# Batch 5's loads requested behind the transpose of the first pairs' last rows, on the same queue

## The chip, the cores and the metric

One core of one Trainium2 chip. The metric is the device time of one execution in microseconds; repeats are given as medians. Each run carries a state: slow when it is over 1.5% above the fastest run of the same kernel, unknown when there is only one.

## The reference, cut to what matters

Linear attention, then an MLP mixer, over 8 batches of 576 rows and 512 columns:

```python
q_p, k_p = phi(q), phi(k)                       # phi(x) = elu(x) + 1
kv  = einsum('bhsd,bhse->bhde', k_p, v)
x   = einsum('bhsd,bhde->bhse', q_p, kv) / den  # attention, 8 heads of 64
u   = x + (relu(x^T w_tok1) w_tok2)^T           # token mixing
out = u + relu(u w_ch1) w_ch2                   # channel mixing, 512 -> 1536 -> 512
```

## The kernel before

The loop runs one pass per batch n. TensorE does the channel mixing of batch n (`mm3`, `mm4`) while, in between, the attention and the token mixing of batch n + 1 and the phi of batch n + 2 are filled in. Each batch has 4 full row groups of 128 and a tail of 64 rows; the tails of two batches share one tile `ut`. Operands that TensorE needs transposed are made by DMA transposes on SyncE's queue: `uT` from `u`, `qT` from phi(q), `uTt` from `ut`. The loads of q, k and v go through the same queue.

```python
def load(nm, n, c, gate=None):                  # 576 KB, two of them for each of q, k, v
    ...
    return after(nc.sync.dma_start(out=raw[nm, n % 2][:, js], in_=src_[:, js]), gate)

def utr_tail_dma(p):                            # "utt"
    nc.sync.dma_start_transpose(out=uTt, in_=ut[p % 2])

def mm3_tail(i):                                # reads uTt, line L517, from step 12 of the next pass
    ...
            nc.tensor.matmul(out=ps[:, m], lhsT=wc1[:, kj, ...], rhs=uTt[:, kj, :], ...)

def nd_mm(n, c, rs):                            # reads qT, line L210, from step 2 of a pass
    ...

AT3 = {..., "mm2t": 15, "uta": 12, "utb": 13, "utt": 15}          # steps in pass n = 2
for n in range(2, B):
    ...
        fill += [(12 + d, lambda: qtr_dma(n + 2))]                # qT, two transposes
        if n == 2:
            fill += [(12 + d, lambda: load_all(5, "qkv"))]        # d = 1 here
        ...
        fill += [(18, lambda: load_all(n + 4, "qkv"))]            # batch 6 in pass 2, 7 in pass 3
    run(big, sorted(fill, key=lambda e: e[0]))
```

So SyncE's order in pass n = 2 is: uT, uT, qT, qT, six loads of batch 5, uTt, six loads of batch 6; pass n = 3 goes on with uT, uT, qT, qT, six loads of batch 7.

Of the kernel before, what the change touches and what calls it, by code (L numbers as in the profile page):

```python
# [18 lines left out]
def kernel(  # L19
# [89 lines left out]
    def load(nm, n, c, gate=None):  # L109
        src_ = src[nm][n].rearrange("(j a) (p t) d -> (a p) j (t d)", a=2, t=T)  # L110
        js = slice(2 * c, 2 * c + 2)
        return after(nc.sync.dma_start(out=raw[nm, n % 2][:, js], in_=src_[:, js]), gate)
# [31 lines left out]
    def phi(nm, n, c):  # L144
        phi_exp(nm, n, 2 * c, 2)
        phi_add(nm, n, 2 * c, 2)
        phi_end(nm, n, 2 * c, 2)
# [49 lines left out]
    def qtr_dma(n):  # L197
        for a in range(2):
            nc.sync.dma_start_transpose(
                out=qT[n % 2][:, 2 * TD * a:2 * TD * (a + 1)].rearrange("p (f s) -> p f s", s=D),  # L200
                in_=qp[half[a]].rearrange("p c t i d -> p (c t i d)"))
# [358 lines left out]
    def mm4_last(cs):  # L560

        p, b, r = B // 2 - 1, 1, R - 1
        m = cs.stop - cs.start
        ps = ps_big.tile([128, 512], FP32, name="h2_ps", tag="big")[:, 0:m]
        for kc in range(NCH):
            nc.tensor.matmul(out=ps, lhsT=cr[b][:, kc, 128 * r:128 * r + 128],  # L566
                             rhs=wc2[:, kc, cs], start=(kc == 0), stop=(kc == NCH - 1))
        o = outp.tile([128, 2, DM], FP32, name="o_sb", tag="o_sb")[:, 0, 0:m]
        nc.vector.tensor_tensor(out=o, in0=ps, in1=u[b][:, r, cs], op=ALU.add)
        for e in range(2):  # L570
            (nc.scalar if e else nc.sync).dma_start(out=outv[2 * p + b, :, 2 * r + e, cs],
                                                    in_=o[half[e]])

    def prep_k(n, g, copy=nc.scalar.copy):
        phi("k", n, g)
        vcast(n, g, copy)

    def load_all(n, nms):
        if n < B:
            for nm in nms:  # L580
                for g in range(2):
                    load(nm, n, g)
# [117 lines left out]
    def steps(n):  # L700

        out_ = [("kv", lambda: kv(n, range(2)))]
        if n == 1:
            puts = [nc.scalar.copy, nc.vector.tensor_copy if n == 1 else nc.scalar.copy]
            out_ += [(f"qt{c}", lambda c=c: qtr(n, c, puts[c])) for c in range(2)]
        for i, rs in enumerate(([0, 1], [2, 3], [4])):
            for g in range(2):
                out_.append((f"nd{i}{g}", lambda g=g, rs=rs: nd(n, g, rs)))
        out_.append(("mm1", lambda: mm1(n)))
        if n > 1:  # L710
            out_ += [("mm2a", lambda: mm2(n, [0, 1])), ("mm2b", lambda: mm2(n, [2, 3]))]
            if n % 2:
                out_.append(("mm2t", lambda: mm2_tails(n // 2)))
            out_ += [("uta", lambda: utr_dma(n, [0, 1])), ("utb", lambda: utr_dma(n, [2, 3]))]
            if n % 2:
                out_.append(("utt", lambda: utr_tail_dma(n // 2)))
        return out_

    def run(bigs, fill):
        for i, big in enumerate(bigs):  # L720
            big()
            for s, fn in fill:
                if s == i:
                    fn()
        for s, fn in fill:
            assert s < len(bigs)
# [16 lines left out]
    fill = [(2, mm2_first_tail)]  # L743
# [24 lines left out]
    fill = [(s, lambda g=g: phi("k", 2, g)) for g, s in ((0, 0), (1, 2))]  # L768
# [11 lines left out]
    for n in range(2, B):  # L780
        p, b = divmod(n, 2)
        if b == 0:
            big = m3(n) + m4(p, [0, 1, 2, 3])
        else:
            big = m3(n) + m3t + m4(p, [4, 5, 6, 7, 8])
            if n + 1 == B:
                big = m3(n) + m3t + m4(p, [8, 4, 5, 6]) + [
                    lambda: mm4_last(slice(0, DM - 128)), lambda: mm4_last(slice(DM - 128, DM))]
        fill = []
        if n + 1 < B:  # L790
            fill += [((AT3 if n == 2 else AT)[nm], fn) for nm, fn in steps(n + 1)]
        if n + 2 < B:
            d = 1 if n == 2 else 0
            fill += [(s + d, lambda g=g: phi("q", n + 2, g)) for g, s in ((0, 8), (1, 9))]
            fill += [(12 + d, lambda: qtr_dma(n + 2))]
            if n == 2:
                fill += [(12 + d, lambda: load_all(5, "qkv"))]
            fill += [(s + d, lambda g=g: prep_k(n + 2, g)) for g, s in ((0, 14), (1, 16))]
            fill += [(18, lambda: load_all(n + 4, "qkv"))]
        run(big, sorted(fill, key=lambda e: e[0]))  # L800
# [29 lines left out]
```

## Time and profile before

| | before |
|---|---|
| time, median of 3 | 263.65 us (263.41 to 263.68) |
| span of the profiled execution | 261.8 us |
| TensorE busy | 252.1 us |
| TensorE's idle time in passes n = 2 and 3 (86.0 to 145.5) | 0.26 us |
| uTt: ready to be requested / requested / landed / first read | 107.87 / 117.47 / 128.8 / 128.8 |

The kernel is bound by TensorE, and transfers matter only where TensorE stands still for one. "The chain" is the work that ended last, followed back from the end of the kernel; its lines give start, duration and what ran (PE is TensorE, SPq is SyncE issuing a transfer, L517 is line 517 of the kernel).

### The profile page before, as it was taken

How to read it: one execution, taken by the hardware profiler on the slowest of the kernel's cores; microseconds unless marked ns; L12 is line 12 of the kernel's file. 1: busy time of each engine (PE TensorE's matmuls, PEld its weight loads, DVE VectorE, ACT ScalarE, POOL GpSimd, SP SyncE). 2: the span in 40 equal slices, each digit the busy share in tenths (PEclk: the TensorE clock that was granted, in tenths of full speed). 3: DMA queues.
4: the chain of work that ended last, by engine and by line, in shares of the span. 5: the costliest groups of instructions: out<-in, count | busy, mean ns of one | idle time of the engine just before them, and what ended most of it. 6: DMA issues, size and time to landing. Idle time of an engine off the chain costs nothing.

```text
span 261.8 us, 5158 instructions
## 1 busy us (share of the span) xinstructions
PE 252.1 (96%) x2102; PEld 132.2 (50%) x2120; DVE 158.9 (61%) x313; ACT 130.9 (50%) x202; POOL 35.7 (14%) x58
## 2 busy tenths in 40 slices
PE   7799999999999999999999999999999999999993
PEld 3584455555744554455554554455554554444642
DVE  5865969966739687948674377939674263420122
ACT  4755773378374468336780468335780453026300
POOL 9760210110001300030001300030001300000000
PEclk9999999999999999999999999999999999999999
DMA  7999999699307994899999990770066500730043
GB/s 256 249 204 278 370 192 377 240 224 410 119 9 141 201 376 187 124 242 382 322 398 229 303 356 3 168 167 20 3 139 115 120 3 2 154 105 3 0 102 98
DMA packets 50087, 48.34 MB, mean 185 GB/s; under 512 B 30288, under 2 KB 35536, under 8 KB 50064
## 3 DMA queue, kind: packets, MB, share of 16 engines
q1 hardware_dynamic: 41904, 35.53, 46.9%
q0 software_dynamic: 7440, 11.44, 20.8%
q10 hardware_dynamic: 720, 1.05, 1.2%
q8 instruction: 16, 0.26, 0.4%
q14 instruction: 7, 0.06, 0.1%
HBM read 35.85 MB, written 9.44 MB: 173 GB/s over the span
## 4 chain that ended last, share of the span: by engine, by line
PE 90%; DMA 3%; ACT 2%; DVE 1%; POOL 1%; issue 1%; ACTq 0%; POOLq 0%
PE h_ps L529 33%; PE c_ps L503 32%; PE a_ps L248 5%; PE c_ps L517 4%; PE h_ps L261 4%; PE nd_ps L210 3%; DMA cr<-in_v_dram 3%; PE kv_ps L169 2%; PE h_ps L566 1%; PE bank L440 1%; POOL qT L610 1%; PE h_ps L282 1%; PE bank L405 1%; PE bank L378 0%; ACT u L303 0%
## 5 line engine op out<-in xcount | busy, mean ns | idle before, releaser
L503 PE MATMUL c_ps<-uT,wc 128*128 128x512 bf16 x384 | 91.4, 379 | 0.0
L510 ACT ACTIVATE cr<-c_ps 128x512 bf16<-128x512 f32 x91 | 53.4, 599 | 75.6 <-PE c_ps L503 75.5
L529 PE MATMUL h_ps<-wc,cr 128*128 128x512 bf16 x363 | 84.3, 379 | 0.5
L529 PEld LDWEIGHTS <-cr 128*128 128x128 bf16 x372 | 35.6, 98 | 41.7 <-issue 1.2
L503 PEld LDWEIGHTS <-wc 128*128 128x128 bf16 x384 | 35.7, 98 | 36.6 <-issue 1.2
L551 POOL DMA_DIRECT2D out_dram<-o_sb x24 | 14.5, 608 | 150.9 <-DVE o_sb L546 150.7
L546 DVE TENSOR_TENSOR o_sb<-h_ps,u 128x512 f32<-128x512 f32 x31 | 21.0, 687 | 21.0 <-PE h_ps L529 20.9
L222 DVE TENSOR_TENSOR x<-nd_ps,den 128x512 bf16<-128x512 f32 (+1 forms) x42 | 25.3, 602 | 1.4
L139 DVE TENSOR_SCALAR e<-e 128x1152 bf16<-128x1152 bf16 x30 | 14.0, 468 | 15.8 <-ACT e L125 15.7
L125 ACT ACTIVATE e<-q_raw 128x1152 bf16<-128x1152 f32 x16 | 18.5, 1160 | 5.7 <-DMA q_raw<-in_q_dram 5.5
L273 DVE TENSOR_TENSOR u<-h_ps,x 128x1024 bf16<-128x1024 f32 x12 | 14.3, 1219 | 10.1 <-PE h_ps L261 10.1
L125 ACT ACTIVATE e<-k_raw 128x1152 bf16<-128x1152 f32 x16 | 18.7, 1169 | 2.3 <-DMA k_raw<-in_k_dram 2.3
L219 DVE TENSOR_SCALAR den<-nd_ps 128x8 f32<-128x8 f32 (+1 forms) x42 | 6.8, 163 | 17.9 <-PE nd_ps L210 17.2
L210 PEld LDWEIGHTS <-qT 128*128 128x128 bf16 x140 | 11.4, 98 | 9.3 <-issue 0.2
L210 PE MATMUL nd_ps<-kvbd,qT 128*128 128x130 bf16 x140 | 15.1, 223 | 0.0
L248 PE MATMUL a_ps<-x,w 128*128 128x512 bf16 x50 | 13.9, 379 | 0.3
L556 DVE TENSOR_TENSOR o_sb<-h_ps,ut 128x512 f32<-128x512 f32 x4 | 2.8, 689 | 18.7 <-PE h_ps L529 18.7
L151 ACT CAST vs<-v_raw 128x1152 bf16<-128x1152 f32 x12 | 13.9, 1160 | 0.0
L251 ACT ACTIVATE ar<-a_ps 128x512 bf16<-128x512 f32 x14 | 7.6, 594 | 11.4 <-PE a_ps L248 11.4
L261 PE MATMUL h_ps<-ar,w2p 128*128 128x512 bf16 x48 | 12.5, 379 | 0.1
L140 DVE TENSOR_TENSOR qp<-e,y 128x1152 bf16<-128x1152 bf16 x16 | 12.1, 759 | 0.6
L131 DVE TENSOR_SCALAR y<-q_raw 128x1152 bf16<-128x1152 f32 x16 | 12.1, 757 | 0.3
(109 smaller groups left out, 221.3 us busy)
## 6 DMA issues: line engine op xcount, KB each, us to landing
k_raw<-in_k_dram SPq DMA_DIRECT2D x16, 576.0 KB, 9.1
q_raw<-in_q_dram SPq DMA_DIRECT2D x16, 576.0 KB, 7.0
v_raw<-in_v_dram SPq DMA_DIRECT2D x14, 576.0 KB, 10.8
out_dram<-o_sb POOLq DMA_DIRECT2D x24, 256.0 KB, 4.5
wc<-in_moe_w_ch_dram POOLq DMA_DIRECT2D x8, 384.0 KB, 9.5
out_dram<-o_sb SPq DMA_DIRECT2D x9, 128.0 KB, 2.3
out_dram<-o_sb ACTq DMA_DIRECT2D x7, 128.0 KB, 2.6
out_dram<-o_sb POOLq DMA_DIRECT2D x6, 128.0 KB, 7.1
```

The lines of the kernel that those rows point to most:

```text
L125: nc.scalar.activation(out=e, in_=f, func=AF.Exp)
L139: nc.vector.tensor_scalar(out=e, in0=e, scalar1=1.0, scalar2=None, op0=ALU.min)
L210: nc.tensor.matmul(out=o[:, a], lhsT=qT[b][:, t0:t0 + 128], rhs=kvbd[b][:, c, a], start=True, stop=True)
L222: nc.vector.tensor_tensor(out=x[b][:, rs[0]:rs[0] + m, HG * D * g:HG * D * (g + 1)].rearrange("p r (h d) -> p r h d", h=HG), in0=v_[:, :, ...
L248: nc.tensor.matmul(out=ps[:, mt], lhsT=w1t[:, b, ms] if r == R else w1[:, r, ms], rhs=x[b][:, r, :], start=(r == 0), stop=(r == R))
L261: nc.tensor.matmul(out=ps[:, i], lhsT=w2v(kt, r, b), rhs=ar[b][:, kt, :], start=(kt == 0), stop=(kt == NT - 1 and not add))
L273: nc.vector.tensor_tensor(out=u[b][:, rs[0]:rs[0] + m], in0=ps[:, 0:m], in1=x[b][:, rs[0]:rs[0] + m], op=ALU.add)
L503: nc.tensor.matmul(out=ps, lhsT=wc1[:, kj, 128 * mc:128 * mc + 128], rhs=uT[b][:, :, kj], start=(kj == 0), stop=(kj == NDM - 1))
L510: nc.scalar.activation(out=cr[b][:, mc, :], in_=ps, func=AF.Relu)
L529: nc.tensor.matmul(out=ps, lhsT=crt[:, kc, :] if t == 8 else cr[b][:, kc, 128 * r:128 * r + 128], rhs=wc2[:, kc, :], start=(kc == 0), stop ...
L546: nc.vector.tensor_tensor(out=o, in0=ps, in1=u[b][:, r, :], op=ALU.add)
L551: (nc.scalar if last and e else put).dma_start(out=outv[2 * p + b, :, 2 * r0 + e:2 * r0 + e + 2 * m - 1:2], in_=live["o"][half[e], 0:m])
```

## The change

The intent: the small transpose of `ut` shall not stand behind 3.5 MB of loads. The whole diff:

```diff
             if n == 2:
-                fill += [(12 + d, lambda: load_all(5, "qkv"))]
+                fill += [(16, lambda: load_all(5, "qkv"))]
```

`utt` is at step 15. In SyncE's program it moves from behind batch 5's six loads to in front of them; the programs of the other four engines stay the same, instruction for instruction.

## The prediction

> **What bounds the kernel now.** I read the page from the top: busy times, the chain that ended last, then the tensor engine's idle time by stretches, and only then the stage that the change touches. The first lines say which engine to watch.
>
> ```profile
> span 261.8 us, 5158 instructions
> PE 252.1 (96%) x2102; PEld 132.2 (50%) x2120; DVE 158.9 (61%) x313; ACT 130.9 (50%) x202; POOL 35.7 (14%) x58
> PE 90%; DMA 3%; ACT 2%; DVE 1%; POOL 1%; issue 1%; ACTq 0%; POOLq 0%
> ```
>
> TensorE (PE) is busy for 252.1 of 261.8 us and makes up 90% of the chain. A change to transfers can only be worth what PE idles because of them, so the next view is busy time by stretch. The number after the comma is PE's busy time; then come the weight loads, VectorE, ScalarE, GpSimd, the granted clock, the DMA share and GB/s.
>
> ```profile
> 0.00:20.00 20.00, 16.26 (x245) 11.12 (x246) 13.56 (x30) 11.62 (x23) 15.14 (x25) 1.00 1.08 235
> 20.00:86.00 66.00, 64.70 (x543) 34.67 (x548) 50.32 (x98) 37.92 (x54) 6.52 (x9) 1.00 0.83 235
> 86.00:145.50 59.50, 59.24 (x473) 29.89 (x477) 40.32 (x79) 31.85 (x47) 7.09 (x12) 1.00 0.99 274
> 145.50:262.00 116.50, 111.95 (x846) 56.51 (x852) 54.69 (x108) 49.48 (x78) 6.97 (x12) 1.00 0.40 101
> ```
>
> The third stretch is the loop's passes n = 2 and n = 3, the only ones that the moved loads can touch directly (the chain has PE start n = 2 at 86.11, n = 3 at 113.45, n = 4 at 145.47). PE idles 59.50 - 59.24 = 0.26 us there, and the clock is full. The start (3.74 us idle) and the last stretch (4.55 us, with the closing eviction and store in it) lie outside the change. What the change moves is SyncE's queue; this is its timeline, start and duration of each issue:
>
> ```profile
> 104.46 2.62 SPq L487 DMA_TRANSPOSE uT<-u  x2
> 107.17 4.18 SPq L199 DMA_TRANSPOSE qT<-qp  x2
> 111.44 2.32 SPq L112 DMA_DIRECT2D q_raw<-in_q_dram  x2
> 113.85 1.81 SPq L112 DMA_DIRECT2D k_raw<-in_k_dram  x2
> 115.71 1.63 SPq L112 DMA_DIRECT2D v_raw<-in_v_dram  x2
> 117.47 3.62 SPq L492 DMA_TRANSPOSE uTt<-ut  x1
> 121.20 2.62 SPq L112 DMA_DIRECT2D q_raw<-in_q_dram  x2
> ```
>
> The three middle lines are batch 5's loads, and the last one begins batch 6's. The transpose of ut (last rows of batches 2 and 3, `utt` in the code) is issued at 117.47, although VectorE finished ut at 107.87 (two writes of L286 from 106.48, 1.39 us together). It stood behind six loads. Its tile, asked for in the window 104 to 150, shows what became of it:
>
> ```profile
> L517 PE MATMUL c_ps<-uTt,wc x48: 217/219/219, 128.8 to 132.3; 128*128 128x128 bf16 x48
> L492 SPq DMA_TRANSPOSE uTt<-ut x1: 3620/3620/3620, 117.5 to 117.5; - x1
> DMA to landing us min/median/max: 11.3/11.3/11.3
> ```
>
> 117.47 + 11.3 = 128.8: it lands in the very moment in which PE first reads it. The chain shows the edge, and beside it the same group of pass n = 5, where nothing stood before the transpose:
>
> ```profile
> 127.96 0.86 PE h_ps L261 x4
> 128.82 1.04 PE c_ps L517 x16
> ...
> 188.10 0.89 PE c_ps L517 x16
> ```
>
> Sixteen equal matmuls take 1.04 us on the chain in n = 3 and 0.89 us in n = 5. The difference, 0.15 us, is what PE plausibly loses to the late transpose. The view of waits fits: of the weight loads, only L517 has an idle entry between 127 and 133 us, 0.3 us once, put down to "issue".
>
> **What the Trainium skill says.** "DMA: Bandwidth & Descriptors", section "Anatomy of one DMA — SWDGE (gpsimd) path", says that DMA engines don't wait on semaphores: waiting is done by the issuing sequencer before dispatch. So a request's place in SyncE's program matters; the trace agrees, since the finished ut had no request out for 9.6 us (107.87 to 117.47). The same page, "Queues, rings and completion order", says that on each DMA engine descriptors are consumed in ring order, although completion isn't strictly in order. The trace agrees as far as it shows this: v's second load was requested at 116.61 and landed about 11.6 us later, near 128.2, and the transpose behind it at 128.8. "Perfetto Trace Analysis", section "DMA Instruction — HWDGE (DVE, Sync)", says that the profiled window of such an issue is descriptor generation, and data movement isn't in it; the trace agrees (3.62 us of issue against 11.3 to landing). So I go by landings, not by issue bars.
>
> **The change, part by part.**
> 1. Removed, added: nothing. The same instructions and bytes, six loads of 576 KB and one transpose; only their order on one queue differs. No compute engine gains or loses work.
> 2. The transpose moves forward. SyncE is through with qT's transposes at 107.17 + 4.18 = 111.35, and ut has been ready since 107.87, so the request goes out at about 111.4 instead of 117.5. In n = 4 and n = 6, without loads before it, its issue takes 1.4 and 1.2 us and its landing 2.8 and 2.5 us. Allowing for qT's second transpose still in flight (it lands 4.5 us after 109.67, at about 114.2), uTt lands at about 114 to 116. It leaves the edge by some 13 us, and PE gains its 0.15 us.
> 3. Batch 5's loads move back by one issue of the transpose: 1.2 to 1.4 us, up to 2.5 if it has to wait for room. First landing before: 111.44 + 7.0 = 118.4. First reader: VectorE's y from q_raw at 123.14, a slack of 4.7 us. The second half of q lands at about 120.6 and is read at 126.2; the first k at about 124.0, read at 131.9; v at about 126.7, first cast at 134.1. The smallest slack, 4.7 us, is above the largest delay that I can construct, 2.5 us. Cost: 0.
> 4. Batch 6's loads, now requested from 121.20, come directly behind batch 5's. Without the transpose's 3.6 us in between, SyncE reaches them at about 111.4 + 1.4 + 6.0 = 118.8 (the six loads take from 111.44 to 117.4 to issue). The DMA share is 1.06 from 113.45 to 128.8, so the engines are full, and earlier requests mostly queue. Batch 6 is first needed in pass n = 4. Value: 0.
> 5. The next transposes on the queue, u and q for pass n = 4, are requested at 130.86 and 137.12 behind batch 6's loads. The last uT lands at about 140.7, 4.8 us before PE's start of n = 4 at 145.47, and the last qT at about 144.8, 4 us before its first matmul at 148.87. The bytes before them are the same, so this slack stays.
>
> Sum: -0.15 us from step 2 and nothing else: 263.65 - 0.15 = 263.5 us. The profiled execution took 263.57 us outside its 261.8 us span, so a difference in the span counts in full.
>
> **The rivals.** A: the transpose wait is larger in unprofiled executions. It lands exactly on the edge, so each microsecond by which the loads before it are slower is a microsecond of PE's idle. For it: the full DMA share. Against it: the three times lie within 0.27 us, and nothing else suggests that the profiled run was lucky. If the loads ran 5% slower (0.05 x 11.3 = 0.6 us), the gain would be 0.7 and the time 262.9.
>
> B: the loads wait for the transpose. In the new order, six loads stand behind a request that depends on VectorE's ut, so a late ut would hold back the whole queue. Against it: ut is done 3.5 us before SyncE arrives (107.87 against 111.35). Should it cost 3 us more than I think, step 3's slack of 4.7 still nearly holds; beyond that, exp and add of q slip, and through ScalarE and VectorE, which also empty PE's banks, perhaps 0.5 us reaches PE: about 264.1.
>
> C: collisions move. Batch 6's loads start some 2 us earlier and share the engines with stores and batch 5's own tail; batch 5's k and v could land a microsecond or two later. Their slack is over 7 us, so the time stays at 263.5.
>
> D: the gain is taken back at the next wait. If PE is 0.15 us earlier, the transposes of pass n = 4 must hold; with 4 us of slack they do, and from there PE runs almost without gaps to the end.
>
> **Range and chances.** The gain is bounded from above by the idle of the stretch, 0.26 us in the profiled run, some tenths more under A, and the loss by slack that is not used up. The spread of repeats (0.27 us) is larger than the effect. I predict 263.5 us, with 8 in 10 between 262.9 and 264.0. A change by 2% is 5.3 us, twenty times the stretch's idle, and nothing in the queue's arithmetic makes 5 us of new waiting: 1% for faster, 98% for within 2%, 1% for slower.
>
> **What would show the steps right or wrong.** Step 2: in the new queue timeline, L492 stands directly behind qT's transposes, at about 111.4, with an issue of 1.2 to 2.5 us and a landing of 2.5 to 5 us; the chain's L517 group in n = 3 falls from 1.04 to about 0.89. Step 3: batch 5's q issue starts at about 112.8 to 113.9, and no wait for q_raw, k_raw or v_raw appears on ScalarE or VectorE. Step 4: batch 6's first load is requested at about 119 to 120. Step 5: PE's idle between 86 and 145.5 is about 0.1 us. The prediction is wrong if PE shows a new wait for uT, qT or kp in n = 3 or n = 4, if L517's gap stays although the transpose landed early (then it was never the cause), or if the time leaves the range.

## The result, and the profile after

| | before | after |
|---|---|---|
| time, median of 4 | 263.66 us (263.41 to 263.92) | 263.34 us (262.89 to 263.99) |
| ratio, 95% interval | | 0.9989 [0.9966, 1.0013] |
| span of the profiled execution | 261.8 us | 262.2 us |

A ratio is the mean time of one kernel's fast runs over that of the other's of the same rounds, so it isn't quite the ratio of the medians quoted beside it. The times can't be told apart. The profiled execution happens to be the slowest of the changed kernel's four, and it shows something that the time alone would hide. Three lines of its page:

```profile
span 262.2 us, 5174 instructions
PE 253.2 (97%) x2120; PEld 132.5 (51%) x2120; DVE 158.8 (61%) x313; ACT 130.9 (50%) x202; POOL 35.6 (14%) x58
PE 77%; DMA 14%; POOL 3%; ACT 2%; SPq 1%; issue 1%; DVE 1%; ACTq 0%; POOLq 0%
```

TensorE is as busy as before, but transfers now hold 14% of the chain instead of 3%. Most of that (27.8 us) lies before 38 us: three loads of weights and q, where nothing changed and where the chain of the kernel before went another way; pass n = 2 starts no later for it (85.98 against 86.11). The other 7.67 us are a transpose of qT, and SyncE's timeline leads to it (start, duration, operation):

```profile
111.38 3.44 SPq L492 DMA_TRANSPOSE uTt<-ut  x1
114.92 1.65 SPq L112 DMA_DIRECT2D q_raw<-in_q_dram  x2
...
120.60 1.86 SPq L112 DMA_DIRECT2D q_raw<-in_q_dram  x2
...
130.73 8.17 SPq L487 DMA_TRANSPOSE uT<-u  x2
138.95 6.32 SPq L199 DMA_TRANSPOSE qT<-qp  x2
```

The same timeline of the kernel before has, for the last two:

```profile
130.86 6.21 SPq L487 DMA_TRANSPOSE uT<-u  x2
137.12 4.94 SPq L199 DMA_TRANSPOSE qT<-qp  x2
```

The transpose goes out at 111.38 instead of 117.47, batch 5's first load at 114.92 instead of 111.44, and the transposes of pass n = 3, twenty microseconds later, take 8.17 + 6.32 us of SyncE instead of 6.21 + 4.94. The tile uTt, in the window 104 to 150, after the change:

```profile
L492 SPq DMA_TRANSPOSE uTt<-ut x1: 3442/3442/3442, 111.4 to 111.4; - x1
DMA to landing us min/median/max: 5.9/5.9/5.9
```

It lands at 111.4 + 5.9 = 117.3, eleven microseconds before its first read. The chain shows the group that had waited, and then where the chain leaves TensorE for a transfer:

```profile
128.70 0.89 PE c_ps L517 x16
...
141.47 7.67 DMA qT<-qp
149.19 0.35 PE nd_ps L210 x3
```

The sixteen matmuls take 0.89 us instead of 1.04. But the last qT, requested at 141.47, lands at 149.1, and TensorE waits for it. In the kernel before the same group of matmuls began on time:

```profile
148.87 0.24 PE nd_ps L210 x4
```

The view of waits of the changed kernel says it in one line, the only wait of TensorE's matmuls between 86 and 200 us:

```profile
PE nd_ps L210 <- DMA qT<-qp: 0.5, 1, 0.5
```

So one wait went and another came. A measure free of the noise of the kernel's start is the stretch on the chain from TensorE's first matmul of pass n = 2 to the matmul behind the first nd group of pass n = 4: 149.11 - 86.11 = 63.00 us before, 149.53 - 85.98 = 63.55 us after. The experiments below show that without any wait it is 62.86 us: 0.14 us lost before, 0.69 after. From there to the end both executions take 112.7 us.

### The profile page after: what moved, and what is told of

It reads as the page before. It is cut to its first block, busy times and chain, and to the rows that moved or that the text cites. A ratio compares the mean times of both kernels' runs of the same rounds, so it can differ in the third digit from the quotient of the medians.

```text
span 262.2 us, 5174 instructions
## 1 busy us (share of the span) xinstructions
PE 253.2 (97%) x2120; PEld 132.5 (51%) x2120; DVE 158.8 (61%) x313; ACT 130.9 (50%) x202; POOL 35.6 (14%) x58
## 4 chain that ended last, share of the span: by engine, by line
PE 77%; DMA 14%; POOL 3%; ACT 2%; SPq 1%; issue 1%; DVE 1%; ACTq 0%; POOLq 0%
PE h_ps L529 28%; PE c_ps L503 27%; DMA wc<-in_moe_w_ch_dram 6%; PE a_ps L248 6%; DMA q_raw<-in_q_dram 5%; PE c_ps L517 4%; PE h_ps L261 4%; PE nd_ps L210 3%; DMA qT<-qp 3%; PE kv_ps L169 1%; PE h_ps L566 1%; SPq L199 1%; ACT e L125 1%; POOL qT L610 1%; POOL cr L117 1%
## 5 line engine op out<-in xcount | busy, mean ns | idle before, releaser
L503 PEld LDWEIGHTS <-wc 128*128 128x128 bf16 x384 | 35.8, 98 | 36.6 <-issue 1.2
L551 POOL DMA_DIRECT2D out_dram<-o_sb x24 | 14.5, 608 | 151.6 <-DVE o_sb L546 151.4
```

The source lines that it names most:

```text
L503: nc.tensor.matmul(out=ps, lhsT=wc1[:, kj, 128 * mc:128 * mc + 128], rhs=uT[b][:, :, kj], start=(kj == 0), stop=(kj == NDM - 1))
L551: (nc.scalar if last and e else put).dma_start(out=outv[2 * p + b, :, 2 * r0 + e:2 * r0 + e + 2 * m - 1:2], in_=live["o"][half[e], 0:m])
```

## The experiments

**Theory (backlog).** The transpose in front makes the loads start 3.5 us later; the loads' tail, and the uT and qT transposes behind it in the queue, land later, and the last qT reaches the moment of its first read. **Rival (chance).** Either kernel meets such a wait now and then, and the late start of the loads has nothing to do with it. A third question came up on the way: the last qT moved by 4.3 us (144.8 to 149.1) though batch 6's last load moved only by 1.8 (137.31 to 139.15). All runs gave correct results.

**e1, e2: both kernels again, unchanged.**

> The kernel before, unchanged, for a second trace and for the size of the noise. Backlog theory (in the changed kernel the six loads of batch 5 go out 3.5 us later, 114.9 instead of 111.4, so that the whole backlog and the qT transposes behind it land later): here the first load of batch 5 is requested at about 111.4, the last qT lands near 145 us and no wait for qT appears in pass n = 4; uTt lands near 128.8. Chance theory (the wait for qT that the changed kernel's profile showed can fall in either kernel): a wait for qT of some tenths of a us may appear here as well. Both: ratio 1.000 within 0.002.

> The changed kernel, unchanged, for a second trace. Backlog theory: batch 5's first load again near 114.9, the last qT lands at 147 to 149.5 us instead of 144.8, so that TensorE waits for it for 0 to 1 us in pass n = 4; the L517 group in pass n = 3 takes 0.89 us; time 263.2 to 264.0. Chance theory: qT lands near 145 us this time and there is no wait; 263.3 us. Ratio 0.998 to 1.001 for both.

e1: 263.55 us, ratio 1.0009 [0.9975, 1.0043]. e2: 264.02 us, ratio 1.0018 [0.9989, 1.0047]. e1's ratio compares a kernel with itself, so its interval (about 0.9 us to either side) is noise alone. Part of it goes with the clock: two of e2's six runs had a mean granted clock of 0.994 and took 264.7 us, the other four (0.998 to 1.0) 263.4 to 264.2. e1's trace again lost time to uTt (0.40 us of the stretch), e2's to qT (0.19):

```profile
148.74 0.41 PE nd_ps L210 x4
```

**e3: the changed kernel, with batch 6's loads behind the qT transposes of pass n = 3.**

```diff
-            fill += [(18, lambda: load_all(n + 4, "qkv"))]
+            if n == 3:
+                fill += [(12, lambda: load_all(6, "qkv"))]
+            if n != 2:
+                fill += [(18, lambda: load_all(n + 4, "qkv"))]
```

> The changed kernel with batch 6's six loads (3.5 MB) moved behind the qT transposes of pass n = 3. Backlog theory: the uT and qT transposes of pass n = 3 find an emptier queue, the last qT lands before 143 us, the wait for qT in pass n = 4 is gone in every execution, the L517 group keeps 0.89 us: 263.1 us, 0.998, with a smaller spread than the changed kernel. Rival (batch 6 and 7 now share one stretch and come late): a wait for q_raw of batch 6 appears on ScalarE in pass n = 4, or the uT transposes of n = 4 are held back: 264 us or more.

263.52 us, ratio 0.9998 [0.997, 1.0025]. In the trace the last qT lands at 140.0, nine microseconds early. The chain:

```profile
147.15 1.83 PE c_ps L503 x8
148.98 0.24 PE nd_ps L210 x4
149.22 0.86 PE c_ps L503 x4
```

No gap, and L517 takes 0.89 us: with its start at 86.36, the stretch is 149.22 - 86.36 = 62.86 us, the floor. The rival's late batch 6 didn't show, nor did the smaller spread that I expected (262.89 to 264.21). By this one trace the backlog of batch 6 is a cause of the late qT; a gain is not shown by the timed runs.

**e4: the transpose issued twice in front of the loads.**

```diff
-                fill += [(16, lambda: load_all(5, "qkv"))]
+                fill += [(16, lambda: utr_tail_dma(1)), (16, lambda: load_all(5, "qkv"))]
```

> The changed kernel with the transpose of ut issued twice before batch 5's loads (the second writes the same bytes again; the result stays right). Backlog theory: batch 5's loads go out another 1.5 to 3.5 us later (116.5 to 118.5), the last qT lands at 150 to 152 us, and TensorE waits 1.5 to 3.5 us for it: 265 to 267 us, 1.005 to 1.013. Chance theory (the loads' start doesn't matter): 263.3 us, 0.999, no longer wait for qT.

264.09 us, ratio 1.0025 [0.9994, 1.0055]. A miss. The second transpose began only when the first had landed (116.6), and batch 5's first load went out at 118.05, 3.1 us later than in the changed kernel, as meant. But batch 6's last load landed at 140.2, only 1.0 us later, and the last qT at 148.1, 0.7 us early: TensorE didn't wait. (VectorE did, 1.2 us for batch 5's q.) A late start of the loads isn't passed on one to one. From the first landing on, one load of 576 KB came every 1.4 us (124.4, 125.8, ...), about 410 GB/s; in the changed kernel the second came 3.4 us behind the first (121.4, 124.8), while a store was in flight that landed at 122.3 (in e4 the same store had landed at 119.2). That the store made the difference is not tested. The simple form of the theory, "later by as much as the loads start later", is wrong.

**e5: the transpose behind batch 6's loads as well.**

```diff
-           ..., "uta": 12, "utb": 13, "utt": 15}      # AT3, from the kernel before
+           ..., "uta": 12, "utb": 13, "utt": 19}
```

> The opposite dose: the kernel before with the transpose of ut put behind batch 6's six loads as well, so that it is requested at about 123 us instead of 117 and has 7 MB of loads before it. Theory of the edge (TensorE's L517 group waits for uTt's landing, and in the kernel before it just touches it): uTt lands behind batch 6's last v, at about 137.5 us instead of 128.8, TensorE stands still from 128.7 to about 137.5, and the time rises by 7.5 to 9 us: 271 to 273 us, 1.029 to 1.034. Rival (a transpose's place on the queue does not set its landing, because it overtakes loads): less than 2 us more.

275.01 us, ratio 1.0398 [1.0366, 1.043], more than expected. uTt landed at 138.2, behind batch 6's last load (137.6), and TensorE waited:

```profile
PE c_ps L517 <- DMA uTt<-ut: 9.1, 1, 9.1
```

That is the wait foretold. The rest is the clock. In the same trace by stretches (busy time of PE, its granted clock, DMA share, GB/s):

```profile
128.00:138.00 10.00, 1.09 (x6) 0.71 1.19 332
138.00:140.00 2.00, 1.77 (x17) 0.50 0.25 54
140.00:142.00 2.00, 2.00 (x9) 0.50 0.00 0
142.00:144.00 2.00, 2.00 (x32) 0.90 0.00 0
```

The clock fell to half at 132.16, during the wait, and came back at 142.40, so TensorE ran at half clock for over 4 us: from L517's start to the matmuls behind the tail it needed 144.21 - 138.23 = 5.98 us against 132.78 - 128.82 = 3.96 in the kernel before, 2.0 us more. 9.1 + 2.0 = 11.1 us, beside the 10.7 us between the medians (275.01 - 264.29).

**e6: batch 6's v loads issued twice.**

```diff
             fill += [(18, lambda: load_all(n + 4, "qkv"))]     # in the changed kernel
+            if n == 2:
+                fill += [(18, lambda: load_all(6, "v"))]
```

> The changed kernel with batch 6's two v loads issued twice (1.18 MB more on the queue, same bytes, result right). Backlog theory by bytes: at about 410 GB/s that is 2.9 us more before the transposes of pass n = 3; the last v lands near 141.5 to 142 instead of 139.1, the last qT at 150.5 to 152 instead of 149, and TensorE waits 2 to 3 us for qT in pass n = 4: 265 to 266.5 us, 1.007 to 1.013. Rival (qT's landing is set by something else, such as the collision with the output stores, as the run with two transposes suggests, whose qT landed at 148.1 although its loads ended 1 us later): qT at 148 to 149, wait under 0.5 us, ratio 0.999 to 1.003.

268.81 us, the median of its three fast runs (the fourth, 272.19 us, was slow; with it 270.01), ratio 1.0142 [1.0094, 1.019]. The experiment did not do what it was for. The second pair writes where the first wrote, so SyncE held it back until the first pair's first load had landed: it stood in front of that request from 130.1 to 139.0. The uT transposes were requested at 140.91 instead of 130.7, the last uT landed at 151.6, and it is uT, not qT, for which TensorE waited:

```profile
PE c_ps L503 <- DMA uT<-u: 4.9, 1, 4.9
```

It says nothing on bytes, but it shows the hazard that my rival B had named for `ut`: a request that waits holds back everything behind it.

**e7: the transpose between batch 5's q loads and its k and v loads.**

```diff
-                fill += [(12 + d, lambda: load_all(5, "qkv"))]
+                fill += [(12 + d, lambda: load_all(5, "q")), (16, lambda: load_all(5, "kv"))]
```

> The transpose of ut between batch 5's q loads and its k and v loads. If the cost of the change is that the DMA engines run short of load bytes while the transpose is issued and runs (164 to 244 GB/s at 116 to 118 us in the changed kernel against 289 to 309 in the kernel before), q's bytes should fill that time: batch 6's last v lands at 137 to 138 instead of 138.6 to 139.1, the last qT at 145 to 147 (no wait), and uTt at 119 to 123 (no wait, L517 group 0.89 us). Time 263.1 to 263.4 at full clock, 0.999. Rival (any transpose between loads costs the same): qT at 148.5 to 149.2 again.

263.70 us, ratio 0.998 [0.9948, 1.0013]. Its trace starts pass n = 2 1.6 us later than the changed kernel's (87.56 against 85.98), so times have to be read from there: the last qT landed 149.3 - 87.56 = 61.7 us after that start, against 63.2, 62.6 and 60.5 in the three traces of the changed kernel. No wait (stretch 62.86), but hardly more slack than the changed kernel: in this trace, placing the transpose behind q doesn't give the time back.

**e8: the transpose of `ut` on TensorE.**

```diff
-                out_.append(("utt", lambda: utr_tail_dma(n // 2)))
+                out_.append(("utt", lambda: (utr_tail if n == 3 else utr_tail_dma)(n // 2)))
```

> The transpose of ut taken off the queue: four TensorE transposes and one ScalarE copy, as pass n = 1 does it. Nothing stands between batch 5's and batch 6's loads. Backlog theory: batch 6's first load goes out at about 117.5 instead of 121, its last v lands at 135 to 136.5, the last qT at 141 to 144: no wait for qT. L517 group 0.89 us. TensorE pays about 0.22 us for the four transposes and gains the 0.15: within 0.2 us of the kernel before, 1.000. Rival (the load rate is limited elsewhere): last v at 137.3 as before.

265.54 us, ratio 1.0037 [1.0012, 1.0062]: 0.4% slower, clear of 1, though under 2%. The queue did as expected or better: batch 6's first load went out at 115.05, its last landed at 135.7, the last qT at 141.6. But I hadn't counted that a transpose on TensorE stands in TensorE's own order. It comes right behind the matmuls that make `ut`, and waits for VectorE:

```profile
PE tp L481 <- DVE ut L286: 1.5, 1, 1.5
```

The stretch is 64.64 us, 1.8 over the floor. What the DMA transpose buys is that nobody waits at that point.

**e9: only batch 6's v loads behind the qT transposes of pass n = 3.**

```diff
+            if n == 3:
+                fill += [(12, lambda: load_all(6, "v"))]
-            fill += [(18, lambda: load_all(n + 4, "qkv"))]     # in the changed kernel
+            fill += [(18, lambda: load_all(n + 4, "qk" if n == 2 else "qkv"))]
```

> The changed kernel with only batch 6's two v loads (1.18 MB) moved behind the qT transposes of pass n = 3: the backlog in front of those transposes is shorter by 1.18 MB, 2.9 us at 410 GB/s, without any new wait of SyncE. Backlog theory: the last load before the transposes lands at 136 to 137 instead of 138.6 to 139.1, the last uT before 141, the last qT at 143 to 146 instead of 148.8 to 149.2, the first nd group of pass n = 4 takes 0.24 us on the chain (it took 0.41 and more in the changed kernel), L517 0.89: both edges clear, 0.15 to 0.5 us better than the changed kernel, ratio to the kernel before 0.998 to 1.000. Rival (the stores alone delay qT): the last qT at 148 or later.

263.73 us, ratio 0.9988 [0.9964, 1.0011]. The last load before the transposes landed at 135.3, the last uT at 138.9, the last qT at 141.4, as early as I wrote or earlier. 1.18 MB less in front (about 2.9 us at 410 GB/s) brought qT 5.7 to 8.4 us forward (counted from the start of pass n = 2), more than its bytes: the qT transposes were requested at 135.29 and 136.66, ahead of the output stores that GpSimd issued at 139.58. That points to the stores, which the next run tests.

**e10: the stores of pass n = 3 that meet the transposes, held back.**

```diff
+                if (p, t) == (1, 5):
+                    live["later"] = store       # the same two stores, 512 KB
+                else:
+                    store()
...
         else:                                   # t == 8
+            if p == 1:
+                live["later"]()
```

> The changed kernel with the two stores (512 KB) that GpSimd issues at 138.8 in pass n = 3 held back behind the next pair, to about 144.5. In the changed kernel the last qT lands 4.0 to 4.4 us later than in the kernel before, while batch 6's last load lands only 1.3 to 1.8 us later; the rest, about 2.5 us, I put down to those stores, whose bytes now meet the transposes. Collision theory: the last uT still lands at 141.5 to 142.5, the last qT at 145.5 to 147, no wait in pass n = 4. Rival (the queue alone): last qT at 148.5 to 149.3 as before the edit. Time within 0.3 us of the changed kernel in both.

263.31 us (263.17 to 263.72), ratio to the kernel before 0.9969 [0.9949, 0.9989]. Batch 6's last load landed at 139.5 and the last uT at 142.7, as late as in the changed kernel; the last qT nevertheless at 145.6, inside the range written for the collision. The timeline of SyncE and the chain:

```profile
131.12 8.12 SPq L487 DMA_TRANSPOSE uT<-u  x2
139.29 3.88 SPq L199 DMA_TRANSPOSE qT<-qp  x2
```

```profile
148.98 0.24 PE nd_ps L210 x4
```

uT still takes 8.12 us, qT 3.88 instead of 6.32, and the wait is gone. So qT was late by two things in a row: the loads' tail pushed the transposes back, and there they ran beside the stores of 512 KB, which by this one trace cost the last qT another 1.2 to 3.9 us (59.3 us after the start of pass n = 2 here against 60.5, 62.6 and 63.2). GpSimd's requests of these stores hardly moved, first in the kernel before, then in the changed one:

```profile
139.09 1.20 POOL L551 DMA_DIRECT2D out_dram<-o_sb  x2 [23.41 <-DVE o_sb L546]
138.82 1.20 POOL L551 DMA_DIRECT2D out_dram<-o_sb  x2 [23.26 <-DVE o_sb L546]
```

This version beats the kernel before by 0.3%, with an interval that excludes 1, though far under 2%; against the changed kernel it was not timed in the same rounds. That the two missing waits are the reason isn't shown: e3, whose trace is free of both as well, came out at 0.9998.

**e11, e12: a third trace of each kernel, one run each.**

> The changed kernel, a third trace, for how often its qT edge costs TensorE something: by the two traces so far the last qT lands at 148.8 to 149.2 and the first nd group of pass n = 4 takes 0.4 us or more on the chain instead of 0.24, and L517's first group 0.89. Chance theory: qT below 147 this time.

> The kernel before, a third trace: uTt lands within 0.2 us of TensorE's first read, L517's first group 1.0 to 1.1 us on the chain, last qT at 144 to 145.5, nd group 0.24 us. If the edge were chance, uTt lands half a us or more away from the read.

e11, 263.95 us: no wait for qT this time; it landed at 147.1, earlier than the 148.8 to 149.2 that I expected. e12, 265.65 us: uTt landed at 130.8, more than a microsecond past the moment when TensorE was ready:

```profile
118.33 12.51 DMA uTt<-ut
130.84 0.04 issue
130.89 1.05 PE c_ps L517 x16
```

All the traces but those of e5 and e6 side by side, in us after TensorE's start of pass n = 2. By the trace of e10, L517 would first read uTt at 42.7 (129.09 - 86.36), and the nd matmuls qT at 62.6 (148.98 - 86.36). The lost time is the stretch less 62.86.

| trace | uTt lands | last load before the uT transposes lands | last qT lands | stretch | lost |
|---|---|---|---|---|---|
| before | 42.7 | 51.2 | 58.7 | 63.00 | 0.14 |
| e1 before | 42.9 | 51.5 | 58.9 | 63.26 | 0.40 |
| e12 before | 43.9 | 52.5 | 59.9 | 64.27 | 1.41 |
| after | 31.3 | 53.2 | 63.2 | 63.55 | 0.69 |
| e2 after | 30.9 | 52.5 | 62.6 | 63.05 | 0.19 |
| e11 after | 30.7 | 52.1 | 60.5 | 62.86 | 0.00 |
| e3 batch 6 later | 30.8 | 42.8 | 53.7 | 62.86 | 0.00 |
| e4 two transposes | 33.6 | 54.1 | 62.0 | 62.86 | 0.00 |
| e7 split | 36.6 | 52.3 | 61.7 | 62.86 | 0.00 |
| e8 on TensorE | | 49.3 | 55.2 | 64.64 | 1.78 |
| e9 v of batch 6 later | 30.9 | 48.7 | 54.8 | 62.99 | 0.13 |
| e10 stores later | 31.2 | 53.1 | 59.3 | 62.86 | 0.00 |

(e9's 0.13 us is lost before 117.5, ahead of the reads of uTt and qT discussed here.) In three traces out of three the kernel before pays at uTt and keeps nearly 3 us or more at qT; the changed kernel never pays at uTt and pays at qT in two of three. How much is paid varies by chance: e12 came out as I had written for that theory (uTt more than half a us past the read), and e11 nearly so (no wait, qT at 147.1, where I had written below 147). Which edge is near is not: in the two kernels uTt lands at 42.7 to 43.9 and at 30.7 to 31.3, qT at 58.7 to 59.9 and at 60.5 to 63.2, without overlap (for qT, three against three would fall this way by luck once in twenty). The losses: 0.14, 0.40 and 1.41 us before, 0.69, 0.19 and 0 after. The averages, 0.65 and 0.29, favour the change by 0.36 us, but three traces each aren't enough to call that measured.

The landing of the last load alone doesn't separate the two kernels (52.5 in e12, 52.1 in e11). Its place against the stores does. In all three traces of the kernel before, the last load landed 1.8 us before the first of the two stores was requested; in the changed kernel's three, 0.7 and 0.4 us before it and 0.3 us behind it, so 1 to 2 us later. In all six the first qT transpose went out 0.2 us before that landing. So the last qT was requested 0.4 to 0.6 us before the first store in the kernel before, and 1.6 to 2.7 us behind it in the changed one. Where it was requested 1.6 to 2.7 us behind (these three and e7), it landed 5.1 to 7.0 us after the last uT; in the other eight traces of the table (e4 among them, 3.5 us behind the store) 2.5 to 4.1 us.

## Why the prediction was right or wrong

The time (263.5 predicted, 263.34 measured), the range and the class held. The mechanism held only in part: the prediction had named a new wait for qT in n = 4 as a sign of being wrong, and that wait came. By its steps:

1. *Nothing removed or added.* Right: only SyncE's order differs.
2. *The transpose leaves the edge, +0.15 us.* Right in the mechanism: request at 111.38 (predicted 111.4), L517 at 0.89 us. Its issue took 3.44 us, not 1.2 to 2.5, and it landed at 117.3, not 114 to 116. I had sized it by passes n = 4 and n = 6, where the next uses weren't near and the queue was emptier. The 0.15 us itself was one draw: rival A, that the wait is larger in other executions, is borne out by 0.40 and 1.41 us.
3. *The loads move back by up to 2.5 us, with 4.7 us of slack.* The move was 3.48 us, since the transpose's issue took longer than any case that I had allowed for. The conclusion held, with less room than 4.7 us: q's halves landed at 121.4 and 124.8, 1.6 and 1.3 us before VectorE read them at 123.02 and 126.10, and no wait for a load appeared.
4. *Batch 6's loads queue up earlier.* They went out at 120.60 rather than 118.8 to 120, and their landings moved 1.7 to 1.8 us later, not earlier. They did no harm to their own readers.
5. *"The bytes before them are the same, so this slack stays."* **This is the step that failed.** The bytes were the same, but not the time: SyncE asked for them 3.5 us later, their tail came 1 to 2 us later against the output stores, and so the last qT went out behind these stores instead of in front of them. A slack of 4 us became about 2 us in one trace (e11) and 0 in another (e2), and was overdrawn by half a us in the first. I had listed the collision with stores as rival C, but looked only at the loads' readers, and dismissed rival D on this very slack.

That the sum came near the truth is partly luck: the two errors offset each other (the old edge cost 0.65 us on average of three traces, not 0.15, and the new one 0.29, not 0), and the difference of the timed kernels is not resolved, so any forecast within a few tenths of 263.5 would have fitted as well.

## What to carry to other kernels

Moving a request forward on an in-order queue moves everything behind it back, and the price can fall a pass later: list the landing and the first read of every transfer that follows, up to the first point where the queue runs empty, and not only of the ones that were swapped. Slack that was measured in one order isn't slack in another, because the other traffic (here the stores) is met at a different moment. When two edges trade places and the time doesn't change, compare several traces from a common point: the median can't show it.

## What the Trainium skill lacked or had wrong

- "Advanced Engine Details and Errata", section "X-Bar Transpose (TRN2)", says that transposing DMAs are as fast as regular ones, with 350 to 400 GB/s to be expected. Here the two uT and two qT transposes of pass n = 2 (1.11 MB in all, by their shapes) took from 104.46 to 114.14 in the kernel before, about 115 GB/s. Up to 110.84, before any store or load was requested, they moved 0.72 MB, 113 GB/s, and never more than 263 GB/s in a fortieth of that time. Loads alone ran at about 410 GB/s.
- No page that I found says how much longer a transposing DMA holds its issuer when requests are outstanding. The same 128 x 512 transpose held SyncE for 1.2 and 1.4 us in passes n = 6 and n = 4, for 2.8 to 3.5 us behind two qT transposes, and for 3.6 to 4.2 us behind six loads. What it waits for stays open; the uT transposes of pass n = 3, behind six loads, let SyncE go on to qT only 0.2 us before the last of these loads landed (all six traces of the two kernels).
- "TensorE: Matmul & The Clock Gate", section "What's actually happening", says that TensorE's clock drops to half after an idle window of about 3.4 us, and comes back after about as long of sustained work. This is confirmed rather than lacking: in e5 (a wait of 9.1 us) the granted clock was 0.50 from 132.16 to 142.40, for over 4 us of work, and that work took 2.0 us longer. So e5's wait cost its own length and this; the waits of 1.3 us in e12 and 1.5 us in e8 left the clock at 1.00.
